# Spreading small transfers over six DMA engines and refilling the gaps around chunk six of a fused attention and spectral mixing kernel

## The chip, the cores and the metric

The program runs on one core of a Trainium2 chip. The metric is the device time of one execution in microseconds, as the median of several runs; every run computes the whole result.

## The reference

Eight sequences of 576 tokens pass through causal attention with eight heads of 64, and the result, seen as 512 channels, passes through a spectral layer. Cut to what matters:

```
cum    = cumsum(max(s, 0))                                   # per head, 576 values
scores = q k^T / 8 + min(cum_k - cum_q, 0), causal
x      = softmax(scores) v                                   # [8, 576, 512]
X      = rfft(x, over the tokens)[first 64 modes]
Y_m    = X_m (w_r[m] + i w_i[m])                             # one 512 x 512 complex product per mode
y      = irfft(Y)
u      = x + y
out    = u + max(u @ w_ch, 0)
```

The weights `w_r` and `w_i` are 64 matrices of 512 x 512 in fp32 each, 134 MB together. They are read once, and turned into bf16 by the transfer.

## The kernel before, in words

**The two stages.** The attention runs in 32 steps `n = (g, b)`: group `g` is one of four pairs of heads, that is 128 of the 512 channels, and `b` is the batch. Each step transposes q and k on TensorE (`transposes`), makes the scores and their exponentials (`scores`), multiplies with v (`av`), and takes the forward transform as a product with a table (`fft`). The running sums of `s` are needed as one more row of the transposed q: `cum_rows` (L336) brings two rows of 576 bf16 values from the DRAM tile `ncum_dram` into one partition of `qt`. SyncE issues these 30 small transfers.

**The weights.** A chunk `c` is eight modes. `modes(g, c)` (L470) multiplies the transformed x of group g with the chunk's weights: 16 products for `ri = 0` (`w_r`) and `ri = 1` (`w_i`), eight each. GpSimd issues all weight transfers in order (`load`, L243), usually 512 KB each and four for a chunk, into a ring of buffers. The products for groups 0 to 2 run between attention steps. Those of group 3, the last, run after attention, chunk by chunk, from 334 us on.

**What follows the last group.** For each chunk of group 3 the sum over groups is `y_sb` (VectorE, L502). `y_transposed` (L698) turns it on TensorE, `y_times_wch` (L706) multiplies with `w_ch` and gives `v_sb`. Both must get from "128 rows of (mode, batch)" into `yv`, with the mode on the partitions. For chunks 0 to 3 and part of 4 and 5 TensorE does it (`gather`); for `v_sb` of chunks 4 to 7 and `y_sb` of chunks 6 and 7 `spread` (L511) does it with a transfer from SyncE: 16 partitions of `yv`, eight pieces of 1 KB each.

**Work that doesn't need the weights.** The 18 output pairs (`pairs`, two tiles of 128 tokens each) need `x @ w_ch`. For 16 of them `keep` (L686) makes this product ahead of time and stores it with ScalarE (L539); six of these are made during attention, and the ten in `late` after it. `work` (L747) does one step of it: it transposes x for the next pair (`x_transposed`, L662: TensorE, then a VectorE copy per tile, through two PSUM buffers) and multiplies the pair before (`x_times_wch`, L677: eight products of 512 columns). The tuple `TAKE` says how many such steps follow each chunk, and `gather` of chunks 0 to 3 does two more. Pairs 0 and 1 stay in PSUM (`z_ps`, four banks, one for each parity and tile) and are finished first.

**The end.** The loop over chunks ends at L880; chunk 6 is L882 to L885. Chunk 7 is called with work between its four blocks of products:

```
yb = modes(NG - 1, NCK - 1, {2: lambda: (first_z(0), first_z(1)), 3: first_u})
```

The first two blocks need `w_r` of chunk 7, block three the first half and block four the second half of `w_i`. `first_z` (L893) adds the inverse transform of chunks 0 to 5 from `yv` and of chunk 6 from `v_sb` to pairs 0 and 1, and `first_u` (L888) does so for u of pair 0. After block four come `y_sb`, its transposition, `v_sb` of chunk 7, and then a written-out list of steps (L952 to L960) that finishes the 18 pairs and stores them. Instructions run on each engine in the order in which the program issues them; there is no scheduler.

Of the kernel before, what the change touches and what calls it, by code (L numbers as in the profile page):

```python
# [10 lines left out]
FP16 = mybir.dt.float16  # L11
BF16 = mybir.dt.bfloat16
# [6 lines left out]
def kernel(  # L19
# [11 lines left out]
    nc = tc.nc  # L31
    B, H, S, D = q.shape
    NM = moe_w_r.shape[0]
    DM = H * D
    P = 128
# [3 lines left out]
    NPAIR = B * H  # L39
    NG = DM // P  # L40
    DT = DM // P
# [4 lines left out]
    MC = 8  # L46
    NCK = NM // MC
# [12 lines left out]
    HP = P // 2  # L60
# [53 lines left out]
    auxpool = aux.enter_context(tc.tile_pool(name="aux_psum", bufs=2, space=PSUM, side="right"))  # L114

    dpool = ctx.enter_context(tc.tile_pool(name="dram", bufs=1, space=bass.MemoryType.DRAM))
    ncum_dram = dpool.tile([NPAIR, S + HP], BF16, name="ncum_dram")
    at = ExitStack()
    ap_ = at.enter_context(tc.tile_pool(name="attn", bufs=1))
    qkpool = at.enter_context(tc.tile_pool(name="qk_sb", bufs=2))  # L120
# [2 lines left out]
    ncum_sb = ap_.tile([NPAIR, S], BF16, name="ncum_sb")  # L123
    NQ = 2
# [211 lines left out]
    def cum_rows(n):  # L336
        if n >= N:
            return
        g, b = divmod(n, B)
        p0 = b * H + 2 * g  # L340
        if n >= 2:
            nc.sync.dma_start(out=qt[n % NQ][D : D + 1, :, :], in_=ncum_dram[p0 : p0 + 2, :S].unsqueeze(0))
            return
        for h in range(2):
            nc.sync.dma_start(out=qt[n % NQ][D : D + 1, h, :], in_=ncum_sb[p0 + h : p0 + h + 1, :])
# [124 lines left out]
    def modes(g, c, meanwhile=None):  # L470


        ps = auxpool.tile([P, DM], FP32, name="yp", tag="aux")
        cols = xs[g % 2].rearrange("p q k h r b m -> p q k (h r b) m")

        def product(ri, q_, cg):
            k0 = HP if ri == 1 and c == 0 and cg == 0 else 0
            nc.tensor.matmul(  # L478
                ps[32 * cg : 32 * cg + 32, :],
                cols[k0:, q_, 1 - ri, :, c * MC // 2 + cg],  # L480
                wt[(g, c, ri)][cg // 2][k0:, 2 * (cg % 2) + q_, :],
                start=(ri == 0 and q_ == 0), stop=(ri == 1 and q_ == 1),
                tile_position=(k0, 32 * cg), skip_group_check=True,
            )

        for x in range(4):
            ri, y = divmod(x, 2)
            if meanwhile and x in meanwhile:
                meanwhile[x]()
            for z in range(4):  # L490
                if meanwhile:
                    product(ri, z // 2, 2 * y + z % 2)
                else:
                    product(ri, y, z)
        if g == 0:
            nc.vector.tensor_copy(out=y_acc[:, c, :], in_=ps)
        elif g < NG - 1:
            nc.vector.tensor_tensor(out=y_acc[:, c, :], in0=ps, in1=y_acc[:, c, :], op=ALU.add)  # L498
        else:
            yb = spool.tile([P, DM], FP16, name="y_sb", tag="y")  # L500
            for cols in halves if c == NCK - 1 else [slice(0, DM)]:
                nc.vector.tensor_tensor(  # L502
                    out=yb[:, cols], in0=ps[:, cols], in1=y_acc[:, c, cols], op=ALU.add
                )
            if c >= NCK - 2:
                spread(c, 0, yb)
            return yb
# [2 lines left out]

    def spread(c, which, rows):  # L511

        nc.sync.dma_start(out=yv[16 * c : 16 * c + 16, :, which, :], in_=rows)

# [65 lines left out]
    with tc.tile_pool(name="sc_psum", bufs=2, space=PSUM) as scpool, \  # L582
            tc.tile_pool(name="tr_psum", bufs=1, space=PSUM) as trpool, \
            tc.tile_pool(name="av_psum", bufs=1, space=PSUM) as avpool:
        cum_rows(0)
        nc.sync.dma_start(out=ncum_dram[:, :S], in_=ncum_sb)
        transposes(0, 0)
        transposes(0, 1)
        load(loads_qk(2) + loads_v(2))
        pad_p()  # L590
        for n in range(N):
            if n in (0, 2):
                nc.vector.memset(xs_flat[n // 2].bitcast(FP32), 0.0)
            tails_due = loads_tails(n // B + 1)[n % B - 3 : n % B - 2] if 2 < n % B < 5 else []
            load((loads_qk(n + LA) if n % 2 else []) + loads_v(n + LA) + tails_due, loads_w(on_chip[n]))
            if n == N // 2 + 1:
                nc.gpsimd.dma_start(out=wch_sb, in_=moe_w_ch.rearrange("(dt p) e -> p dt e", p=P))
            cum_rows(n + 1)
            scores(n, 0)
            av(n - 1, 1)  # L600
            if n and n % B == 0:
                scores(n, 1)
                fft(n - 1)
                av(n, 0)
                mode_products(n, 0)
                transposes(n + 1, 0)
                mode_products(n, 1)
                transposes(n + 1, 1)
                continue
            mode_products(n)  # L610
            transposes(n + 1, 0)
            scores(n, 1)
            i = first_pairs[n - N + len(first_pairs)] if n >= N - len(first_pairs) else None
            if i is not None:
                first_transposed(i, 0)
            transposes(n + 1, 1)
            fft(n - 1)
            av(n, 0)
            if i is not None:
                first_product(i, 0)  # L620
                first_transposed(i, 1)
            if i is not None:
                first_product(i, 1)
        av(N - 1, 1)
        fft(N - 1)
# [11 lines left out]
    for b in range(4):  # L637
# [8 lines left out]
        old[:, i * 2 * DM : (i + 1) * 2 * DM].bitcast(FP16).rearrange("p (x t c) -> p x t c", x=2, c=P)  # L646
        for i in range(2)
    ]

    places = [finpool.tile([P, 4 * DM], BF16, name="r_sb", tag="r", bufs=3) for i in range(2)]  # L650
    places += [finpool.tile([P, 4 * DM], BF16, name=f"z1_{i}") for i in range(NLOC)]
# [8 lines left out]
        return [(slice(NL * i, NL * i + NL), b + i, ident16h[:NL, :NL]) for i in range(2)]  # L660

    def x_transposed(i):  # L662
        xts[i] = xt_sb[len(xts) % 2]
        for x, (b, T) in enumerate(pairs[i]):
            ps = upool.tile([P, DT, P], FP32, name="xt_ps", tag="u")
            for rows, bb, ident in parts(b, T):
                for dt in range(DT):
                    nc.tensor.matmul(
                        ps[:, dt, rows], x_all[: rows.stop - rows.start, dt, bb, T, :],
                        ident, start=True, stop=True, skip_group_check=True,  # L670
                    )
            nc.vector.tensor_copy(out=xts[i][:, x], in_=ps)
# [1 line left out]
    def start_z(i, x):  # L674
        zs[i, x] = zpool.tile([P, DM], FP32, name="z_ps", tag=f"z{i % 2}{x}")

    def x_times_wch(i, last):  # L677
        for x in range(2):
            start_z(i, x)
            for dt in range(DT):  # L680
                nc.tensor.matmul(  # L681
                    zs[i, x], xts[i][:, x, dt, :], wch_sb[:, dt, :],
                    start=(dt == 0), stop=(last and dt == DT - 1), skip_group_check=True,
                )

    def keep(i):  # L686
        x_times_wch(i, True)
        j = late.index(i)
        kept_place(i, places[j])
        for x in range(2):  # L690
            keep_product(i, x, zs.pop((i, x)))
# [6 lines left out]
    def y_transposed(yb, c=NCK):  # L698
        ps = auxpool.tile([P, DT, P], FP16, name="yt_ps", tag="aux")
        for dt in range(DT):  # L700
            nc.tensor.transpose(ps[:, dt, :], yb[:, bass.ts(dt, P)], ident16h)
        yt = yt_first[:, :, c % NY, :] if c < NCK - 2 else spool.tile([P, DT, P], FP16, name="yt_sb", tag="yt")
        nc.scalar.copy(out=yt, in_=ps)
        return yt

    def y_times_wch(c, yt):  # L706
        vp = auxpool.tile([P, DM], FP32, name="v_ps", tag="aux")
        for dt in range(DT):
            nc.tensor.matmul(
                vp, yt[:, dt, :], wch_sb[:, dt, :], start=(dt == 0), stop=(dt == DT - 1)  # L710
            )
        vb = spool.tile([P, DM], FP16, name="v_sb", tag="v")
        nc.vector.tensor_copy(out=vb, in_=vp)
        spread(c, 1, vb)
        return vb
# [41 lines left out]
            keep(i)  # L757

    late = [i for i in kept if i not in first_pairs]
    order_z = list(late)  # L760
    TAKE = (3, 2, 4, 0, 0, 0)
    us, rs = {}, {}
    last = len(pairs) - 1
    x_pool = ()
# [97 lines left out]
    for c in range(NCK - 2):  # L862
        yb = modes(NG - 1, c)
        for x in range(TAKE[c] - 1):
            work()
        if c == NCK - 3:
            x_transposed(0)
        yt = y_transposed(yb, c)
        if TAKE[c]:
            work()  # L870
        if c >= NY:
            if c == NCK - 3:
                x_times_wch(0, False)
                x_transposed(1)
            y_times_wch(c, yt)
            if c == NCK - 3:
                gather(NY, NCK - 2, (), (0,))
                x_times_wch(1, False)
        elif c == NY - 1:
            gather(0, NY, (1, 3), (1, 0))  # L880
    assert not order_z and not ahead
    c = NCK - 2  # L882
    yb6 = modes(NG - 1, c)
    yt = y_transposed(yb6)
    vb6 = y_times_wch(c, yt)  # L885


# [108 lines left out]
```

## Time and profile before

| what | value |
|---|---|
| median of 3 runs (range) | 441.62 us (440.95 to 442.1) |
| the profiled execution: time, span | 442.11 us, 440.3 us |
| mean granted TensorE clock | 0.925 |
| busy: TensorE, VectorE, ScalarE, GpSimd | 77%, 57%, 51%, 39% |
| HBM read, over the span | 163.58 MB, 393 GB/s with the writes |
| weight transfers of 512 KB, issue to landing | 13.6 us (`w_r`), 13.2 us (`w_i`) |
| chain that ended last: DMA, TensorE, VectorE | 53%, 25%, 15% |

The span runs from the first to the last instruction; the execution takes 1.8 us more than that. A DMA share of 1.1 in a window means that the 16 engines are busy throughout, since consecutive packets overlap a little. PEclk is the clock that TensorE was granted, 1.00 being full speed. The chain is followed back from the last instruction, so its shares say what ended the waits, not what an engine did in total.

### The profile page before, as it was taken

To read this page: it belongs to the slowest core of one execution; us is meant where nothing else is said; L and a number is where in the kernel's file an instruction comes from. 1 tells how busy PE (TensorE), PEld (TensorE's weight loads), DVE (VectorE), ACT (ScalarE), POOL (GpSimd) and SP (SyncE) were. 2 spreads that over 40 slices of the span, in tenths; PEclk is the share of its full clock that TensorE was granted. 3 is DMA by queue.
4 is the path that set the end of the run, shared out by engine and by line. 5 is a ranking of instruction groups with operands and counts; after the bars stand their busy time and mean duration, and the time that the engine had idled before them with its cause. 6 is when DMAs were issued, how large, how long until landed. Compare 5 with 4: busy or idle time off the path is not lost.

```text
span 440.3 us, 10592 instructions
## 1 busy us (share of the span) xinstructions
PE 340.8 (77%) x4409; PEld 203.7 (46%) x4409; DVE 252.5 (57%) x574; ACT 226.0 (51%) x421; POOL 171.7 (39%) x257
## 2 busy tenths in 40 slices
PE   1588999899695977973939458899987797778995
PEld 1365666465463644641616125556554345432341
DVE  7667776677573555752715315766655344450795
ACT  1387878267463634860727024766651334330794
POOL 6555454424353444323444343433322212310293
PEclk9999999999988888995968767999999989996999
DMA  9999999999999999999999999999999999996498
GB/s 179 207 206 206 204 206 208 207 209 207 207 205 207 210 207 210 207 209 208 205 209 208 209 208 209 207 210 206 210 211 212 212 211 211 203 218 121 155 381 347
DMA packets 69063, 93.30 MB, mean 212 GB/s; under 512 B 25932, under 2 KB 27592, under 8 KB 69016
## 3 DMA queue, kind: packets, MB, share of 16 engines
q0 software_dynamic: 61424, 81.28, 104.6%
q1 hardware_dynamic: 7592, 11.36, 7.2%
q8 instruction: 34, 0.56, 0.5%
q14 instruction: 13, 0.11, 0.1%
HBM read 163.58 MB, written 9.51 MB: 393 GB/s over the span
## 4 chain that ended last, share of the span: by engine, by line
DMA 53%; PE 25%; DVE 15%; issue 3%; POOL 2%; ACT 1%; DVEq 0%; POOLq 0%
DMA w_sb<-in_moe_w_i_dram 21%; DMA w_sb<-in_moe_w_r_dram 17%; DMA qk<-in_k_dram 8%; DMA qk<-in_q_dram 5%; PE sc_ps L397 3%; DVE xs L468 3%; DVE qt L359 3%; PE z_ps L681 3%; PE yp L478 3%; DVE x_all L443 2%; PE av_ps L433 2%; PE sc_ps L391 2%; PE tr_ps L355 2%; DVE xt L553 2%; PE z_ps L773 2%
## 5 line engine op out<-in xcount | busy, mean ns | idle before, releaser
L405 ACT ACTIVATE p_sb<-sc_ps,cumt_sb 128x576 f16<-128x576 f32 (+1 forms) x256 | 141.9, 636 | 21.8 <-PE sc_ps L397 21.4
L397 PE MATMUL sc_ps<-qt,kt 128*128 128x512 bf16 (+2 forms) x384 | 76.8, 312 | 6.9 <-ACT kt L359 6.1
L243 POOL DMA_DIRECT2D v<-in_v_dram x72 | 51.4, 714 | 60.6 <-DMA w_sb<-in_moe_w_i_dram 12.8
L243 POOL DMA_DIRECT2D w_sb<-in_moe_w_i_dram x62 | 38.5, 623 | 89.2 <-DMA w_sb<-in_moe_w_i_dram 28.3
L359 DVE COPY qt<-tr_ps 64x576 bf16<-64x576 bf16 x64 | 47.8, 747 | 41.5 <-PE tr_ps L355 41.5
L478 PE MATMUL yp<-w_sb,xs 128*32 128x512 bf16 (+1 forms) x480 | 42.2, 431 | 29.1 <-DMA w_sb<-in_moe_w_i_dram 25.4
L355 PE MATMUL tr_ps<-ident,qk 64*64 64x64 bf16 x1152 | 34.3, 205 | 33.8 <-DMA qk<-in_k_dram 16.0
L243 POOL DMA_DIRECT2D w_sb<-in_moe_w_r_dram x60 | 37.4, 624 | 53.0 <-DMA w_sb<-in_moe_w_r_dram 33.3
L397 PEld LDWEIGHTS <-kt 128*128 128x128 bf16 x384 | 38.3, 105 | 34.5 <-ACT kt L359 12.8
L391 PE MATMUL sc_ps<-negm,ident 128*128 128x256 bf16 x256 | 53.5, 293 | 0.1
L355 PEld LDWEIGHTS <-qk 64*64 64x64 bf16 x1152 | 26.4, 117 | 51.7 <-DVE kt L359 20.3
L376 ACT ACTIVATE p<-sc_ps,cumt 128x64 f16<-128x64 f32 x32 | 10.1, 314 | 73.8 <-PE sc_ps L372 73.6
L433 PE MATMUL av_ps<-v,p_sb 128*128 128x65 f16 x1024 | 44.2, 197 | 1.8 <-DVE x_all L443 0.6
L359 ACT COPY kt<-tr_ps 64x576 bf16<-64x576 bf16 x32 | 22.8, 714 | 40.8 <-DVE qt L359 40.1
L433 PEld LDWEIGHTS <-p_sb 128*128 128x128 f16 x1024 | 37.4, 100 | 9.6 <-DVE x_all L443 5.4
L468 DVE CAST xs<-ft_ps 64x128 bf16<-64x128 f32 x128 | 36.7, 287 | 7.3 <-PE ft_ps L458 5.7
L478 PEld LDWEIGHTS <-xs 128*32 128x32 bf16 (+1 forms) x512 | 17.8, 146 | 46.0 <-DMA w_sb<-in_moe_w_i_dram 24.6
L438 DVE TENSOR_REDUCE den<-av_ps 128x5 f32<-128x10 f32 x64 | 10.8, 169 | 48.3 <-PE av_ps L433 47.3
L443 DVE TENSOR_TENSOR x_all<-av_ps,rcp 128x320 f16<-128x320 f32 x64 | 31.5, 492 | 2.2
L498 DVE TENSOR_TENSOR y_acc<-yp,y_acc 128x512 f32<-128x512 f32 x16 | 11.1, 692 | 29.2 <-PE yp L478 28.5
L539 ACT COPY z<-z_ps 128x512 f32<-128x512 f32 x22 | 12.9, 586 | 26.9 <-PE z_ps L571 14.2
L458 PE MATMUL ft_ps<-Ff_sb,x_all 128*64 128x192 f16 (+1 forms) x320 | 24.4, 266 | 1.0 <-DVE x_all L443 1.0
(107 smaller groups left out, 439.4 us busy)
## 6 DMA issues: line engine op xcount, KB each, us to landing
w_sb<-in_moe_w_r_dram POOLq DMA_DIRECT2D x60, 512.0 KB, 13.6
w_sb<-in_moe_w_i_dram POOLq DMA_DIRECT2D x55, 512.0 KB, 13.2
out_dram<-r_w SPq DMA_DIRECT2D x16, 512.0 KB
v<-in_v_dram POOLq DMA_DIRECT2D x72, 64.0 KB, 11.1
qk<-in_q_dram POOLq DMA_DIRECT2D x15, 288.0 KB, 12.0
qk<-in_k_dram POOLq DMA_DIRECT2D x15, 288.0 KB, 13.2
x_all<-in_moe_w_r_dram POOLq DMA_DIRECT2D x4, 512.0 KB, 8.4
w_sb<-in_moe_w_i_dram POOLq DMA_DIRECT2D x3, 384.0 KB, 12.7
```

The source lines that it names most:

```text
L243: nc.gpsimd.dma_start(out=dst, in_=src)
L355: nc.tensor.transpose(ps[rows, r, :], src[rows, r, :], ident16[rows, rows])
L359: copy(out=to[:, :, :, half * RH : half * RH + RH], in_=ps[HP * i : HP * i + HP].rearrange("d r (h p) -> d h p r", h=2),)
L391: nc.tensor.matmul(ps[:, bass.ds(w * S, W)], ident16, negm[:, bass.ts(r, W)], start=True, stop=False, skip_group_check=True,)
L397: nc.tensor.matmul(ps[:, c0 : c0 + i1 - i0], keys[:, w, r, :], qh[:, i0:i1], start=False, stop=True, skip_group_check=True,)
L405: nc.scalar.activation(out=pt[:, poff[x] : poff[x] + S - w * W], in_=ps[:, w * S : (w + 1) * S - w * W], func=ACTF.Exp, bias=cumt_sb[:, x, ...
L433: nc.tensor.matmul(ps[:, I, r : r + NCH], lhsT, rhs, start=(i == 0), stop=(i == len(todo) - 1), skip_group_check=True,)
L443: nc.vector.tensor_tensor(out=x_all[:, g, b, :, D * h : D * h + D], in0=ps[:, :, 1 : NCH], in1=rcp.unsqueeze(2).to_broadcast([P, NT, D]), ...
L458: nc.tensor.matmul(ps[HP * q_ : HP * q_ + HP].rearrange("p h f -> p (h f)"), x_all[:nT, g, b, T, q_::2], Ff_sb[:nT, T, :], start=(T == 0), ...
L468: nc.vector.tensor_copy(out=xs[g % 2][HP * h : HP * h + HP, q_, :, h, :, b, :], in_=a)
L478: nc.tensor.matmul(ps[32 * cg : 32 * cg + 32, :], cols[k0:, q_, 1 - ri, :, c * MC // 2 + cg], wt[(g, c, ri)][cg // 2][k0:, 2 * (cg % 2) + ...
L681: nc.tensor.matmul(zs[i, x], xts[i][:, x, dt, :], wch_sb[:, dt, :], start=(dt == 0), stop=(last and dt == DT - 1), skip_group_check=True,)
```

## The change

It has two parts.

**Transfers.** `ncum_dram` is laid out as three pieces of 192 values per row, so that `cum_rows` moves six runs of 384 bytes instead of two of 1,152. `spread` cuts the 16 partitions of chunks 4 and 5 into three transfers of 6, 6 and 4 partitions; those of chunks 6 and 7 stay whole. By the change's own words these transfers then go over six DMA engines (pieces of 6 partitions or runs over six, the piece of 4 over four); two runs went over two, and 16 partitions over 16.

**Order.** One kept product, that of pair 17 (`late[-1]`), leaves the steps after chunk 2 (`TAKE[2]` goes from 4 to 3). Its transposition goes behind the products of chunk 5, ahead of that of pair 0, and its product with `w_ch` between the `w_r` blocks and the `w_i` blocks of chunk 6. The product of pair 1 moves from the end of chunk 5's part into chunk 6: one tile before the transposition of `y_sb`, one behind it. A third buffer, `xt_x`, holds transposed x. Giving `modes` a `meanwhile` also changes the order of chunk 6's products: two column groups at a time instead of four.

```diff
-    ncum_dram = dpool.tile([NPAIR, S + HP], BF16, name="ncum_dram")
+    NE6 = 6
+    CP = 2 * S // NE6
+    ncum_dram = dpool.tile([NPAIR, S // CP, CP + 32], BF16, name="ncum_dram")
...
-            nc.sync.dma_start(out=qt[n % NQ][D : D + 1, :, :], in_=ncum_dram[p0 : p0 + 2, :S].unsqueeze(0))
+            nc.sync.dma_start(
+                out=qt[n % NQ][D : D + 1, :, :],
+                in_=ncum_dram[p0 : p0 + 2, :, :CP].rearrange("h x t -> (h x) t"),
+            )
...
     def spread(c, which, rows):
-        nc.sync.dma_start(out=yv[16 * c : 16 * c + 16, :, which, :], in_=rows)
+        cuts = (0, 2 * MC) if c >= NCK - 2 else (0, NE6, 2 * NE6, 2 * MC)
+        for r0, r1 in zip(cuts, cuts[1:]):
+            nc.sync.dma_start(
+                out=yv[2 * MC * c + r0 : 2 * MC * c + r1, :, which, :], in_=rows[B * r0 : B * r1, :]
+            )
...
-        nc.sync.dma_start(out=ncum_dram[:, :S], in_=ncum_sb)
+        nc.sync.dma_start(
+            out=ncum_dram[:, :, :CP], in_=ncum_sb.rearrange("c (x t) -> c x t", t=CP)
+        )
...
+    xt_sb.append(finpool.tile([P, 2, DT, P], FP16, name="xt_x"))
...
-        xts[i] = xt_sb[len(xts) % 2]
+        xts[i] = xt_sb[len(xts) % 3]
...
-    def x_times_wch(i, last):
-        for x in range(2):
+    def x_times_wch(i, last, xx=(0, 1)):
+        for x in xx:
...
-    order_z = list(late)
-    TAKE = (3, 2, 4, 0, 0, 0)
+    order_z = late[:-1]
+    TAKE = (3, 2, 3, 0, 0, 0)
...
         if c == NCK - 3:
+            x_transposed(late[-1])
             x_transposed(0)
...
                 gather(NY, NCK - 2, (), (0,))
-                x_times_wch(1, False)
...
-    yb6 = modes(NG - 1, c)
+    yb6 = modes(NG - 1, c, {2: lambda: keep(late[-1])})
+    x_times_wch(1, False, (0,))
     yt = y_transposed(yb6)
+    x_times_wch(1, False, (1,))
     vb6 = y_times_wch(c, yt)
```

## The prediction

> **What bounds the kernel now.** I read the busy slices first. DMA is at 9 in every slice until 396 us, so the weights set the pace, and then there is a tail of 35 us. Second, the chain of waits around the hand-over, in order of time (start, length, what):
>
> ```profile
> 383.57 15.64 DMA w_sb<-in_moe_w_r_dram
> 399.21 0.14 issue
> 399.35 1.09 PE yp L478 x6
> 400.44 0.96 PE z_ps L773 x2
> 401.41 0.85 PE z_ps L784 x2
> 402.26 0.99 PE z_ps L773 x3
> 403.25 0.85 PE z_ps L784 x3
> 404.11 1.00 PE yp L478 x4
> 405.11 0.57 PE u_ps L803 x2
> 405.68 0.43 PE u_ps L773 x2
> 406.12 0.43 PE u_ps L784 x2
> 406.55 0.60 PE yp L478 x4
> 407.15 0.02 issue
> 407.17 0.44 DVE y_sb L502
> ```
>
> The `w_r` transfers of chunk 7 land at 399.21. From there TensorE, not DMA, holds the chain to the last products at 406.5. Two matmuls of 512 columns (L773) cost 0.96 at 400.44 and 0.43 at 405.68. Third, windows of 1 us and of one clock interval show why (PE, PEld, DVE, ACT, POOL busy; PEclk; DMA share; GB/s):
>
> ```profile
> 391.50:394.92 3.42, 2.22 (x21) 0.74 (x18) 2.38 (x4) 1.33 (x3) 0.00 (x0) 1.00 1.12 217
> 394.92:398.33 3.41, 1.43 (x8) 0.53 (x8) 1.08 (x2) 0.59 (x1) 0.00 (x0) 1.00 1.12 215
> 398.33:401.74 3.41, 2.39 (x12) 0.68 (x12) 0.00 (x0) 0.00 (x0) 0.00 (x0) 0.50 1.01 201
> 401.74:405.16 3.42, 3.42 (x15) 0.86 (x14) 0.00 (x0) 0.00 (x0) 0.00 (x0) 0.50 0.32 67
> ...
> 401.00:402.00 1.00, 1.00 (x3) 0.15 (x1) 0.00 (x0) 0.00 (x0) 0.00 (x0) 0.50 0.74 130
> 402.00:403.00 1.00, 1.00 (x5) 0.36 (x6) 0.00 (x0) 0.00 (x0) 0.00 (x0) 0.50 0.53 116
> 403.00:404.00 1.00, 1.00 (x6) 0.18 (x2) 0.00 (x0) 0.00 (x0) 0.00 (x0) 0.50 0.30 66
> 404.00:404.80 0.80, 0.80 (x6) 0.19 (x4) 0.00 (x0) 0.00 (x0) 0.00 (x0) 0.50 0.07 13
> ```
>
> TensorE was busy for 1.43 of 3.41 us ahead of 398.33, and then had half its clock until 405.16. And DMA does not stop at once: its share falls from 1.1 to 0.07, about one engine of 16, over 4 us. The engines reach the end of the same stream at different times; the last weights land at 404.80. Fourth, the queue table of the page names a load that isn't even:
>
> ```profile
> q8 instruction: 34, 0.56, 0.5%
> ```
>
> 34 packets take 0.5% of 16 x 440.3 us, 35 us, or 1.0 us each. 0.56 MB over TensorE's 8,818 instructions is 64 bytes each, so I take them for fetches of its code. Their lengths in the trace's DMA records repeat with a period of eight (974, 961, 893, 892, 948, 945, 935, 974 ns), so I read eight engines in turn, each made late by some 4 us. Between 354 and 384 us the completions of 512 KB transfers form 16 series with a step of 2.486 us each, which is an engine at its own limit, not a shared one. At 325 to 330 us these series stand in two groups: eight within 2.3 us of the earliest, eight 2.8 to 4.6 us behind it.
>
> **Part 1, the transfers.** A spread costs each of 16 engines eight packets of 1 KB. These took 59 ns in the records, less 19 ns by which consecutive packets overlap: 8 x 0.040 and a completion, 0.35 us. By the queue row of SyncE (7,592 packets, 7.2%, 67 ns each) it would be 0.53. Two spreads leave the late engines, if these are not among the six: the end of the weights moves from 404.8 to 404.1, and `w_r` of chunk 7 from 399.2 to 398.5. Bounds: if the late engines are among the six, they get 16 packets more per spread, 2 x 16 x 0.040 = 1.3 us later; at best 2 x 0.53 = 1.1 us earlier. I take 0.7 earlier: around the last running sum, at 310.0, which goes over the two engines of the old layout, two series that stretch by 61 ns belong to the early group. This places two of the six; the other four I assume.
> The running sums: 30 x 2 packets of 1,152 bytes, 61 ns each by those series, become 30 x 6 of 384 bytes, 22 ns (the records of the 384-byte pieces of the table loaded at the start) to 44 with a completion. Two engines save 30 x 17 to 39 ns, 0.5 to 1.2 us, four others gain 0.7 to 1.3; these are ahead of the late ones by more than that. Nobody waits for these rows (the list of who held up TensorE names transposes and ScalarE, no transfer of `qt`), so this costs nothing unless they come a whole step, 6.6 us, later. The store into `ncum_dram` has 12 packets per engine x 22 ns instead of 4 x 64: equal. SyncE issues four more transfers at 0.55 us each; queued behind them are the next spreads, whose data comes 4 us later, and the stores: nothing. `v_sb` of chunk 7 reuses chunk 5's buffer and so waits for three pieces (399.2 below, written at 406): nothing.
> A row weighed against a rule: the DMA share above falls over 4 us, so dealing evenly over 16 would keep the late ones late. The Trainium skill (DMA: Bandwidth & Descriptors, Rules for kernel authors) speaks against the change: it asks for an outermost dimension that is a multiple of 16, since a smaller one confines a transfer to as many engines. By the rule alone the 0.7 would be 0, and the sum 1.6.
>
> **Part 2, the order.** The kept product leaves the stretch after chunk 2: 0.45 (xt_ps) and 1.73 (z_ps) on the chain, 2.2 us. Chunk 5 started at 383.38 without a wait for data. Its weights: chunk 6's last wait ended at 393.91; four transfers of 2.486 are 9.94, a fetch 1.0 and a spread 0.35 lie between: 382.6. So of the 2.2 only 0.8 is gained there; the rest turns into waiting for weights.
> Chunk 5 then gets two more transposes. TensorE's part is 0.6, but four tiles pass two buffers, each freed by a VectorE copy of 0.65 behind `y_sb` (0.69): `x_times_wch(0)`, queued behind the waiting transposes with `y_sb`'s own, starts 2.85 us after the products, not 1.4. The gather ends at 390.5 - 0.8 + 1.4 = 391.1, and the 1.9 of pair 1 is gone from there. Chunk 6: `w_r` products, two groups at a time, 0.9, to 392.0; the kept product 1.73, to 393.7, over the time in which TensorE waited 0.79 for `w_i`; `w_i` products to 394.6; pair 1's first tile 0.86 under `y_sb` (0.80 waited before); the second under ScalarE's copy (0.68 waited before); `v_ps` 1.04, to about 397.8. `v_sb` follows at 398.5; `first_z` needs it only at 400.
> So the interval ahead of the hand-over holds nearly 3 us of work instead of 1.43, and the idle stretch before chunk 7 is 0.7 instead of 1.87. With the clock kept: `w_r` 398.5 + 0.14; 0.9 of products; `first_z` at half its 3.65, 1.85; block three 0.5; `first_u` 1.3: 403.2. Block three finds its half of `w_i` (two transfers of 1.25 before the last: 401.6) just there. Block four then waits for the weights at 404.1 + 0.1 = 404.2, against 406.48: **2.3 us**. That is the next late thing: without part 1's 0.7 it is 404.9, 1.6 us. With half the clock it is 398.5 + 7.13 (406.48 - 399.35) = 405.6, 0.9 us.
> Does the clock stay? Row: 1.43 busy of 3.41 halved it; 391.50 to 394.92 had 2.22 busy and did not. Between these I take the nearer, 2.22, for an interval with 2.2 or more in any phase. The intervals run on their own grid, so a run may fall otherwise.
> The Trainium skill (TensorE: Matmul & The Clock Gate, Part 1) has the gate throttle after an idle window of 3.4 us; here the window wasn't idle, so the row goes further than the rule. By the rule there would have been no loss to win back, and the sum would be part 1 alone.
> From block four on the tail is the same instructions, TensorE bound with its clock up in both, so the gain passes 1:1. ScalarE's two more copies (0.59 each) in chunk 6 lie in its idle time (it waited 3.4 and 2.1 us there); they free the banks of pair 1 at 393.5 and 394.3, ahead of 394.6. Without that cover pair 1 would come up to 0.6 later, within the 1.0.
>
> **Sum.** The profiled execution took 442.11 (440.3 and 1.8 around it), 0.5 above the median. 442.11 - 2.3 = 439.8; from the median it is 439.3. Some of the runs before may have kept their clock, which would explain their 1.15 us of spread, so I stay near the first: **439.7**.
>
> **Rivals.** A measurement tells 0.3%, 1.3 us, from no change.
> (a) The six engines are no help or only the clock is won: 1.6 us, 440.0 to 440.5. For it: no row gives the engine of a packet.
> (b) The clock halves anyway: 0.9 us, 440.8 to 441.2. For it: 2.39 busy of 3.41 did not bring it back at 401.74.
> (c) The six engines include late ones: weights end at 404.8 + 1.3 = 406.1, block four 0.3 earlier than before: 441.3 to 441.8.
> (d) Slower: the spread of chunk 5 becomes the late one. Its three pieces put 24 packets on four engines, each between two weight packets of 0.154: 24 x 0.19 = 4.6 us from 394.6 (issue 390.7, and 3.9 us from issue to packets, as the spreads at 384.2 and 395.3 show): 399.2, when `first_z` wants it at 399.6. It decides from 400.6 on (the 1.0 by which block four waits anyway). With one packet per two of the weights it is 24 x 0.35 = 8.3, 402.9; TensorE stands still for over 3 us, the clock halves, and `first_z` 3.65, block three 1.07 and `first_u` 1.45 end at 409.1: +2.6, 444.2 from the median. Against it: packets alternate one for one in the records at 400.
>
> **How the numbers follow.** The forecast gets 0.48, (a) 0.18, (b) 0.12, (c) 0.08, (d) 0.14. Faster by over 0.3% (under 440.3): the forecast and half of (a), 0.57. Within: half of (a), (b), (c), 0.29. Slower: 0.14. The range goes from 438.8 (part 1 at 1.1, from the median: 441.62 - 2.7) to 441.9, past (c); (d) is outside. The forecast's own range is 438.8 to 440.3.
>
> **What would show it.** Right: PEclk 1.00 from 395 to 405; L773 at 0.43 per two; a wait of block four for `w_i` of about 1 us; the last weights at 404.1, with the DMA share steeper; a small wait ahead of chunk 5. Wrong: a wait of L773 for `yv` (d); 0.50 in PEclk (b); weights that end at 404.8 or later (a, c); new waits for `qt` in the attention steps.

## The result, and the profile after

The change makes the kernel slower: 443.16 us (median of 22 runs, 441.38 to 445.27) against 441.74 us (22 runs of the kernel before beside it). The ratio is 1.003, with a 95% interval of 1.0019 to 1.0041: 0.8 to 1.8 us. The forecast of 439.7 and its range up to 441.9 both miss it. The profiled execution took 443.24 us, with a span of 441.5 and a mean clock of 0.913, close to the median.

The chain of waits of the kernel after, at the places shown of before (start, length, what):

```profile
347.29 15.89 DMA w_sb<-in_moe_w_i_dram
...
363.22 0.69 PE yp L483 x8
...
392.33 0.42 PE g_ps L740 x16
...
402.88 0.60 PE yp L483 x8
403.48 0.54 PE z_ps L785 x2
404.02 0.43 PE z_ps L796 x2
404.45 0.55 PE z_ps L785 x4
405.01 0.43 PE z_ps L796 x4
405.44 0.58 PE yp L483 x4
406.02 0.54 PE u_ps L815 x2
...
407.43 0.60 PE yp L483 x4
408.05 0.44 DVE y_sb L507
```

From 363.22 on no piece of this chain is a weight transfer. Block four, which began at 406.55 before, begins at 407.43, and it waits for TensorE: the last weights landed at 404.5 by the trace's DMA records (404.8 before). The two products of L773, now L785, cost 0.54 instead of 0.96, so the clock is up at the end, as forecast, and yet the end is 0.9 us later. The windows show what came ahead of that (PE, PEld, DVE, ACT, POOL busy; PEclk; DMA share; GB/s):

```profile
361.00:364.34 3.34, 1.27 (x17) 0.36 (x16) 0.41 (x1) 0.59 (x1) 1.22 (x2) 1.00 1.14 213
364.34:374.58 10.24, 8.26 (x49) 5.35 (x50) 4.16 (x7) 2.81 (x6) 1.22 (x2) 0.50 1.12 211
374.58:395.06 20.48, 15.06 (x164) 8.77 (x162) 10.00 (x17) 7.04 (x13) 4.83 (x8) 1.00 1.08 203
395.06:398.47 3.41, 3.00 (x13) 0.95 (x14) 1.73 (x3) 0.85 (x3) 0.00 (x0) 0.50 1.13 216
398.47:408.00 9.53, 9.53 (x62) 3.38 (x60) 1.38 (x2) 1.70 (x3) 0.00 (x0) 1.00 0.56 118
```

In this execution the clock halves at two other places, from 364 to 375 and from 395 to 398, and each time TensorE holds the chain. Which intervals fall so differs between executions; that alone is no cause. What the change does to the time had to come from runs with its parts taken singly.

### The profile page after: what moved, and what is told of

It reads as the page before. It is cut to its first block, busy times and chain, and to the rows that moved or that the text cites. A ratio compares the mean times of both kernels' runs of the same rounds, so it can differ in the third digit from the quotient of the medians.

```text
span 441.5 us, 10548 instructions
## 1 busy us (share of the span) xinstructions
PE 340.1 (77%) x4362; PEld 205.1 (46%) x4409; DVE 252.6 (57%) x574; ACT 226.1 (51%) x421; POOL 171.3 (39%) x257
## 4 chain that ended last, share of the span: by engine, by line
DMA 44%; PE 30%; DVE 17%; issue 3%; ACT 3%; POOL 2%; DVEq 0%; POOLq 0%; ACTq 0%
DMA w_sb<-in_moe_w_i_dram 18%; DMA w_sb<-in_moe_w_r_dram 16%; DMA qk<-in_k_dram 5%; PE yp L483 5%; DVE qt L364 4%; PE z_ps L693 4%; DVE xs L473 3%; PE sc_ps L402 3%; DMA qk<-in_q_dram 3%; PE tr_ps L360 2%; DVE x_all L448 2%; PE av_ps L438 2%; PE sc_ps L396 2%; DVE kt L364 2%; PE g_ps L740 2%
## 5 line engine op out<-in xcount | busy, mean ns | idle before, releaser
L402 PE MATMUL sc_ps<-qt,kt 128*128 128x320 bf16 (+2 forms) x337 | 65.2, 297 | 10.7 <-ACT kt L364 5.8
L364 DVE COPY kt<-tr_ps 64x576 bf16<-64x576 bf16 x32 | 24.4, 762 | 0.4
```

What stands on the lines that cost most here:

```text
L364: copy(out=to[:, :, :, half * RH : half * RH + RH], in_=ps[HP * i : HP * i + HP].rearrange("d r (h p) -> d h p r", h=2),)
L402: nc.tensor.matmul(ps[:, c0 : c0 + i1 - i0], keys[:, w, r, :], qh[:, i0:i1], start=False, stop=True, skip_group_check=True,)
```

## The experiments

All were timed in five rounds beside the kernel before. Differences in us are the ratio less one, times the median of before in the same rounds; in brackets the 95% interval. The ratio takes in every execution, so it need not follow the medians where single executions are long (`order_spreads` below). Each profile is of one execution.

**Each part alone.** `order_only` has the second part (order) and the transfers of before; `transfers_only` the running sums and both spreads, with the order of before.

```diff
# transfers_only, beside the new layout of ncum_dram
-        nc.sync.dma_start(out=yv[16 * c : 16 * c + 16, :, which, :], in_=rows)
+        cuts = (0, 2 * MC) if c >= NCK - 2 else (0, 6, 12, 2 * MC)
+        for r0, r1 in zip(cuts, cuts[1:]):
+            nc.sync.dma_start(out=yv[2 * MC * c + r0 : 2 * MC * c + r1, :, which, :], in_=rows[B * r0 : B * r1, :])
# order_only
-    order_z = list(late)
-    TAKE = (3, 2, 4, 0, 0, 0)
+    order_z = late[:-1]
+    TAKE = (3, 2, 3, 0, 0, 0)
...
-    yb6 = modes(NG - 1, c)
+    yb6 = modes(NG - 1, c, {2: lambda: keep(late[-1])})
+    x_times_wch(1, False, (0,))
     yt = y_transposed(yb6)
+    x_times_wch(1, False, (1,))
```

> Only the running sums and the spreads of chunks 4 and 5 go over six engines; the order of the work is that of before. Theory O (the order costs the time: with the kept product gone from the stretch after chunk 2 TensorE waits for the weights of chunk 3, its clock halves during the gather, and it never again gets ahead of the weights): 0 to 0.5 us faster than before, since the last weights land a little earlier (404.4 against 404.8 in the two profiles). Theory T (the transfers cost it: the attention ended 0.46 us later in the changed kernel, first products of the last group at 334.63 instead of 334.17): 1.0 to 1.5 us slower.

> Only the order is changed: the kept product of pair 17 from chunk 2 to chunk 6, and pair 1 into chunk 6; the transfers are those of before. Theory O: 1.2 to 2.0 us slower than before, with a half clock from about 364 us on and no wait of TensorE for weights after chunk 3. Theory T: 0.5 us faster to no change, and chunk 7 waits for its weights.

Measured: `transfers_only` 444.17 us, +2.6 (+1.6 to +3.5); `order_only` 440.82, -0.9 (-1.8 to -0.1). The order helps, and the transfers cost more than it brings, and more than theory T expected. In `order_only` the clock stayed up over the hand-over, and the chain ends on the weights, as the forecast had it for part 2 alone:

```profile
394.92:398.33 3.41, 3.41 (x25) 1.36 (x23) 1.39 (x2) 1.52 (x3) 0.00 (x0) 1.00 1.15 221
398.33:401.74 3.41, 2.93 (x19) 1.08 (x18) 0.69 (x1) 0.59 (x1) 0.00 (x0) 1.00 0.99 191
```

```profile
388.20 17.48 DMA w_sb<-in_moe_w_i_dram
405.68 0.04 issue
405.72 0.67 PE yp L478 x4
```

In `transfers_only` TensorE starts on the `w_r` of chunk 7 at 400.53 instead of 399.35, and behind their products there is a gap that the profile puts down to nothing:

```profile
383.89 16.51 DMA w_sb<-in_moe_w_r_dram
400.40 0.14 issue
400.53 1.09 PE yp L480 x6
401.62 0.57 issue
402.20 1.01 PE z_ps L779 x2
```

L779 is the inverse transform in `first_z`, which reads `yv`. The trace's semaphore events, by which each DMA engine reports that its share of a transfer has landed (sixteen for a whole spread, six for a piece of six partitions), explain the gap: the last piece of chunk 5's spread is complete at 402.00. This is the first sign of rival (d).

**The smallest piece of the order.** `pair1_moved` only moves the product of pair 1 into chunk 6 and leaves the kept product where it was.

```diff
-                x_times_wch(1, False)
...
+    x_times_wch(1, False, (0,))
     yt = y_transposed(yb6)
+    x_times_wch(1, False, (1,))
```

> Only the product of pair 1 moves into chunk 6, on both sides of the transposition of y_sb; the kept product stays behind chunk 2, the transfers are those of before. Theory O: chunk 3 is as before, TensorE waits some 2.5 us for the weights of chunk 6 instead of 0.8 and the product fills the 0.7 behind it; 0.5 us faster to 0.5 us slower, depending on whether the clock stays up through that wait. Theory T: the same. The third reading: 1 to 1.5 us slower.

Measured: 440.68 us, -0.8 (-1.5 to -0.2), no worse than the whole order. Its profiled execution had half the clock from 392.4 to 399.2 and still began block four at 405.08. The other half, the kept product moved without pair 1 (`keep_moved`), has no time: pair 17 needs the two banks of `z_ps` that pair 1 then still holds, and the engines wait for each other for ever.

**Which of the transfers.** `sums_only` has the running sums over six engines, `spreads_only` the two spreads in pieces of 6, 6 and 4, `spreads_eight` the two in two pieces of 8 (`cuts = (0, 8, 2 * MC)`).

> The two spreads in three pieces (6, 6 and 4 partitions), running sums and order as before. So far: both transfer edits together cost 2.4 us (441.8 to 444.17), with the last w_r of chunk 7 at 400.53 instead of 399.21 and the last weights at 405.46 instead of 404.80. Theory S (the six engines include the late ones: 16 packets of 1 KB more per spread on these at 0.04 us, 2 x 16 x 0.04 = 1.3 us, and the pieces of chunk 5 come late for first_z): slower by 1.5 to 2.4 us, w_r of chunk 7 at 400.2 or later. Theory R (the running sums in six packets of 384 bytes cost it): within 0.5 us of before, w_r of chunk 7 at 399.2 to 399.6.

> The running sums and their store in runs of 384 bytes over six engines, spreads and order as before. Theory S: within 0.5 us of before (four engines gain 30 x 22 to 44 ns = 0.7 to 1.3 us, two lose 0.5 to 1.2), w_r of chunk 7 at 399.0 to 399.6. Theory R: slower by 1.5 to 2.4 us, and w_r of chunk 7 at 400.2 or later.

> A dose between: the two spreads in two pieces of 8 partitions, which puts 16 packets on each of eight engines instead of 24 on four and 16 on two (before: 8 on each of sixteen). Theory S: an engine that is late gets 8 packets more per spread instead of 16, so about half of the loss of the three pieces, slower by 0.6 to 1.2 us, w_r of chunk 7 about 0.6 later than before. Theory R: within 0.5 us of before.

Measured: `sums_only` 441.66, +0.3 (-0.2 to +0.8); `spreads_only` 442.81, +1.5 (+0.8 to +2.1); `spreads_eight` 442.55, +1.4 (+0.7 to +2.1). The spreads cost it. Two pieces cost about as much as three, which the dose of theory S did not foresee. The landing of `w_r` of chunk 7, on which theories S and R are also set, tells nothing: in the profiles of all runs it is at 398.79 to 400.40 with split spreads and at 398.69 to 400.37 without.

**Which spread.** `split_four` cuts only chunk 4's spread (`c != NCK - 4` keeps the others whole), `split_five` only chunk 5's (`c != NCK - 3`).

> Only the spread of chunk 4 in three pieces (6, 6, 4); it is through by 392, and first_z reads it at 400, so it cannot be late for a reader. Theory W: half of the loss of both spreads, +0.4 to +0.9 us. Theory L (chunk 5's spread, late for first_z, costs it): within 0.3 us of before.

> Only the spread of chunk 5 in three pieces. With chunk 4's at 0.0 and both at +1.3, chunk 5's alone should cost +0.9 to +1.5 under theories W and L alike; a smaller cost (under 0.5) would say that the two spreads only cost together, by what they add up to on the same six engines.

Measured: `split_four` 441.46, 0.0 (-0.5 to +0.5); `split_five` 443.72, +1.9 (+1.0 to +2.9). Chunk 5's carries it all, and by its middle more than was expected. Its chain, and one row of the list of who held up TensorE, name the wait:

```profile
390.71 0.77 SPq L515
391.48 0.05 issue
391.52 9.58 DMA yv<-v_sb
401.10 0.05 issue
401.15 1.04 PE z_ps L777 x2
```

```profile
PE z_ps L777 <- DMA yv<-v_sb: 0.6, 1, 0.6
```

The last piece is issued at 391.5 and `first_z` gets it at 401.1. The DMA records show how: the sixteen engines of before finished this spread together, at 395.5 to 396.2. Here six finish the first piece at 395.4 to 396.2, six the second at 397.5 to 398.3, four the third at about 399.2 to 399.9 (the records don't name the engine, so single packets can belong to the next spread). That is one packet of 1 KB in 0.21 to 0.25 us, which fits a turn with about one weight packet. Another 1.2 us pass until the last of the four engines reports the landing, at 401.10; the whole spread of before had landed at 396.42, 0.3 behind its last packet. The wait of 0.6 that the trace shows is a part of the 1.9: this execution, at 442.91, is 0.8 under its run's median.

**Is it the six engines' load?** `load_six` keeps the spreads whole and lets two more transfers follow each, 6 x 8 packets of 1 KB into spare DRAM; `load_sixteen` the same 96 KB over all sixteen; `load_five` has those of `load_six` behind chunk 5 only; `tiny_five` two transfers of 16 x 64 bytes behind chunk 5.

```diff
         nc.sync.dma_start(out=yv[16 * c : 16 * c + 16, :, which, :], in_=rows)
+        if c < NCK - 2:                                   # load_five: c == NCK - 3
+            for r0 in (0, 6):
+                nc.sync.dma_start(out=spare[c % 2, r0 : r0 + 6, :B, :DM], in_=rows[B * r0 : B * (r0 + 6), :])
```

> The two spreads stay whole over sixteen engines; two more transfers of 6 x 8 packets of 1 KB follow each of them, into spare DRAM that nobody reads: 16 packets more on each of six engines, twice. Theory W (the six engines include those that set the landing of the weights; 2 x 16 x 0.04 = 1.3 us): slower by 0.8 to 1.6 us, as the spreads in pieces were (+1.25). Theory L (the pieces are only late for first_z, or hold up the spreads behind them, and the weights do not mind): the copies also stand ahead of the later spreads in SyncE's queue, so within 0.6 us of before, and the last weights within 0.3 of 404.8.

> The same two extra transfers per spread and the same 96 KB as load_six, into spare DRAM, but each over all sixteen engines (6 packets more on each instead of 16 on six). Theory W (the load of the six engines costs it): the latest engine gets 2 x 6 x 0.04 = 0.5 us, so +0.2 to +0.6, less than half of load_six (+1.0). Rival (the number of transfers or their bytes cost it, whatever the engine): +0.8 to +1.2, as load_six.

> The two extra transfers on six engines follow chunk 5's spread alone; all spreads stay whole, so no reader gets its rows late. Theory W, with the place that split_four points to (only what comes late in the stream counts): +0.7 to +1.2, as load_six. Theory L (lateness of chunk 5's own pieces): 0 to +0.3.

> The kernel before with two more transfers behind chunk 5's spread, of 16 packets of 64 bytes each, into spare DRAM that nobody reads: transfers without bytes. If the number of transfers costs it (SyncE's queue, its rings): +0.7 to +1.2 us as with load_five. If it is the bytes: 0.0 within 0.4.

Measured: `load_six` 442.55, +1.3 (+0.7 to +1.9); `load_sixteen` 443.0, +1.3 (+0.7 to +2.0); `load_five` 442.28, +0.9 (+0.2 to +1.7); `tiny_five` 442.44, +0.6 (0.0 to +1.1). The same bytes cost the same on six engines and on sixteen, so theory W, that the choice of engines delays the weights, falls; it fell with `split_four` already. But theory L did not foresee a cost of the copies either, since nobody waits for them. An estimate by bytes fits the intervals of the three copies: 96 KB at the 216 GB/s of the windows is 0.45 us for each spread. That a transfer without bytes costs nothing isn't settled by `tiny_five`. The change adds no bytes to the spreads, but like `tiny_five` it puts two more transfers behind chunk 5's first, so part of what its split costs may be due to their number, a rival that stays open (`split_four` adds two as well, behind chunk 4's, and cost nothing).

**Inside the change.** `order_sums_six` is the change without the split spreads, `order_spreads` without the new running sums, `after_whole_five` without chunk 5's split alone:

```diff
-        cuts = (0, 2 * MC) if c >= NCK - 2 else (0, NE6, 2 * NE6, 2 * MC)
+        cuts = (0, 2 * MC) if c >= NCK - 3 else (0, NE6, 2 * NE6, 2 * MC)
```

> The change without its spreads: the new order and the running sums over six engines. Theory S (the spreads alone cost): as the order alone, 440.8, which is 0.5 to 1.2 us faster than before. Rival (running sums and order together cost, as running sums and spreads together seemed to cost 0.9 more than the sum of the two alone): 441.5 or above.

> The change without its running sums: the new order and the spreads in pieces. Theory S: nearly the whole loss against the order alone, 442.1 to 443.2, slower than before by 0.5 to 1.5 us. Rival (the running sums carry most of it inside the change): 441.0 to 441.6, faster than before or the same.

> The whole change except that chunk 5's spread stays one transfer over sixteen engines. Theory L (the last piece of chunk 5's spread reaches first_z at about 401 instead of 397): the loss goes, to what the order with the running sums had, 440.7 to 441.6, at or below before. Rival (the loss comes from all parts together): 442.3 or above, at most a third of the 1.5 us gone.

Measured: `order_sums_six` 441.01, -0.2 (-0.8 to +0.3); `order_spreads` 441.20, +0.4 (-0.4 to +1.1); `after_whole_five` 441.51, 0.0 (-0.5 to +0.6), inside what theory L expected. Leaving chunk 5's spread whole takes the change from +1.3 to nothing. `order_spreads` missed what theory S expected of it: its median lies in the rival's range, under the 441.55 of before beside it, and its ratio is above one through single executions of up to 444.30. Its profile, of its fastest execution, shows the late piece again, with TensorE early and its clock up:

```profile
399.15 0.67 PE yp L478 x8
399.82 1.00 issue
400.82 0.59 PE z_ps L778 x2
```

The third piece's packets end at about 399.6 there, and it has landed at 400.62 by the semaphore events, 0.2 before 400.82. `after_whole_five` has no such gap, and its chain ends on the weights, as in `order_only`:

```profile
388.49 17.09 DMA w_sb<-in_moe_w_i_dram
405.57 0.04 issue
405.62 0.67 PE yp L483 x4
```

**The parts added up.** The runs hold every combination of the three parts. In the four pairs that differ by one part alone, the split spreads add 1.5, 2.3, 1.3 and 1.5 us, the running sums 0.3, 1.1, 0.7 and 0.9, and the order -0.9, -0.5, -1.1 and -1.3. The means, 1.65, 0.75 and -0.95, add up to the change's +1.3 within 0.2, so the parts seem to act each by itself. If the intervals are independent, each mean is good to about 0.5 (an estimate from the intervals above).

**What the clock is worth.** `before_fill7` and `before_fill4` add eight and four matmuls of 512 columns behind `v_ps` of chunk 6 to the kernel before; nobody reads them.

```diff
     vb6 = y_times_wch(c, yt)
+    filler(1, 8)          # before_fill4: 4
```

> The kernel before with eight more matmuls of 512 columns, whose result nobody reads, after v_ps of chunk 6, in the time in which TensorE waits for w_r of chunk 7: 1.7 us at full clock. It tells what the clock alone is worth at the end. Theory C (the interval with 1.43 us busy of 3.41 halves the clock, which then costs the chain): PEclk 1.00 from 398 to 405, block four waits for its weights at about 404.9 instead of starting at 406.55, faster by 1.0 to 1.6 us. Rival (the end is set by the transfers, whose last lands at 404.80, and the clock hides behind them; or the added products push w_r's own): within 0.5 us of before or slower.

> The kernel before with four more matmuls of 512 columns (0.9 us at full clock) after v_ps of chunk 6, result unread. Theory C (the halved clock ahead of chunk 7 costs the chain): 34 code fetches as before, PEclk 1.00 from 398 to 405 in most runs, faster by 0.6 to 1.5 us. Rival (clock hidden behind the transfers): within 0.4 us of before.

Measured: 442.38, +1.2 (+0.6 to +1.8), and 441.96, +0.8 (-0.1 to +1.6). The expectation failed in the time, but not at its place. In the profile of `before_fill7`, its fastest execution, the clock was up from 399.5 on:

```profile
400.37 0.60 PE yp L478 x8
400.97 0.54 PE z_ps L781 x2
...
404.91 0.60 PE yp L478 x4
...
434.00 0.60 DVEq L1000
```

Block four begins at the forecast 404.9, and the last piece of the chain, on VectorE's queue, starts at 434.00 instead of 435.65. But the queue table counts one more fetch:

```profile
q8 instruction: 35, 0.57, 0.5%
```

By the records it runs for 1.43 us at 430.8, amid the last stores. In the last microsecond of these 13 packets follow one another, as on one engine, where in before 139 end, and the stores end at 439.0 (439.1 before). So the 1.6 us that the clock brought went to an engine that was late with the end. That the fetch made it late is argued, since the records don't name the engine. `before_fill4` has 34 fetches within its span, but its profiled execution, at 445.68 us, is the slowest of its twelve and says nothing of the usual one. In it the four matmuls did not keep the clock, which was halved from 396.5 to 403.4.

## Why the prediction was wrong

**Part 1, the transfers: the step that failed.** It gave the two spreads a gain of 0.7 us, with bounds of -1.1 to +1.3, because packets leave the late engines. Measured alone they cost 1.5 us, past the upper bound by its middle (the interval, 0.8 to 2.1, takes it in), and chunk 5's alone 1.9. No gain in the weights appeared: their last landing lies between 403.6 and 405.5 in the runs with split spreads, at 404.8 in before. The assumption that the six engines are not the late ones found no support either: where chunk 4's pieces pass in `transfers_only`, the two latest of the series of completions stretch and nine others keep their step of 2.486 us. But by `split_four` even that costs nothing that could be measured.

**Rival (d) named the place and got 0.14.** Its price for one packet in turn was 24 x 0.19 = 4.6 us from 394.6, so 399.2, and it decides only from 400.6 on; so I took the rows of the spread to come in time. Two terms were too small. Packets took 0.21 to 0.25 us each (394.6 to 399.6 in `order_spreads`, 393.9 to 399.9 in `split_five`). And the end of the packets was taken for the arrival, with 1.0 to 1.2 us missing in these two runs. With both, 24 x 0.23 + 1.2 = 6.7 from 394.6 gives 401.3, beyond that point. The price of 2.6 us lies inside the interval of `split_five` by luck: it took the piece to come at 402.9 and TensorE to stand still for over 3 us, and measured were 401.1 and 0.6.

The Trainium skill (DMA: Bandwidth & Descriptors, Anatomy of one DMA) puts a fixed cost of some 2.0 us on a transfer issued by GpSimd, most of it the wait for the write's receipt behind the last byte. The 0.3 to 1.2 us between last packet and landing here, on transfers of SyncE, agree in kind and are smaller. The rule cited against the change (same page, Rules for kernel authors) was the better guide: each piece of six partitions shows landings from just six engines.

**The running sums** were priced at nothing: +0.3 alone, not told from zero. Yet in all four pairs that differ by them alone the run that has them is slower, by 0.75 on the mean, so nothing was probably too low. Where this arises no run shows.

**Part 2, the order,** was right in kind. Forecast without part 1: 1.6 us, block four waiting for weights at 404.9. Measured: 0.9 (0.1 to 1.8), waiting for weights at 405.7, as the last of them came 0.6 later in that execution. So the end of the weights is one mis-sized term. A step ahead of it was wrong: the 1.9 us of pair 1 is not "gone from there". In before, its product (390.50 to 392.40) ran while VectorE copied the gathered rows out of PSUM, and the products of chunk 6 need these buffers. Without it TensorE waits just as long, and the `w_r` products of chunk 6 begin at 393.99 in `order_only` (forecast 391.1) and at 395.47 in the change. The rows of `order_only` and of the change:

```profile
PE yp L478 <- DVE yv L739: 1.9, 1, 1.9
PE yp L483 <- DVE yv L750: 1.9, 1, 1.9
```

`order_only` had room for this, since block four waited for weights anyway; the change had not. One sum is off by a little too: 441.62 - 2.7 is 438.9, not 438.8.

**The clock** was expected to stay up where the interval ahead of the hand-over is filled. It did in the profiled executions of `order_only`, `order_spreads` and `after_whole_five`. It did not in that of the change (395.06 to 398.47) and, with 0.56 and 0.58 from 394 to 398, in that of `order_sums_six`, where the intervals fell otherwise. So rival (b)'s mechanism is there in some executions. Nor is 2.2 us of work in an interval enough in any phase: in the change's execution 2.45 us from 333.60 to 337.03 were followed by half the clock.

**In the changed kernel itself** the late piece hides behind a late TensorE. Chunk 5's `v_sb` is written 3.0 us later than before (392.38 against 389.35), after the half clock of 364 to 375 and the added transposes; the packets of its spread run from 397.2 to 402.3, and its last piece has landed at 403.07 by the semaphore events. `first_z` begins at 403.42, without a wait for it. So with the spread issued when it was, a TensorE that was in time could have begun at most 0.4 us earlier. That is worked out, not shown by a run.

**What stays open.** Why two pieces of eight partitions cost 1.4 us: in the one profile, the fastest of its twelve runs, they are not late for a reader (landed at 397.83, read at 399.68). In the profile of `spreads_only` too the last piece lands at 400.51, ahead of `first_z` at 401.17. So the wait is shown in three profiles (`transfers_only`, `split_five`, `order_spreads`, 0.6 to 1.0 us each), and what the split costs beyond it, the number of transfers perhaps, is not. And how much of the change's loss is the late piece, how much the two clock stretches: `after_whole_five` gives back 1.3 us, and `order_only` stands 0.9 further down, with intervals that touch.

**The version that beats both** is the order alone (440.82) or only pair 1 moved (440.68), with the spreads left over sixteen engines.

## What to carry to other kernels

Price a small transfer by the arrival of its last packet at its reader, not by the bytes that it takes from others: packets on its fullest engine, times the turn that each takes beside the bulk stream, and the time until its landing is reported (0.3 to 1.2 us here). Cutting a transfer that someone waits for into pieces for fewer engines lengthens just that. And when a gain at a place vanishes at the end, look for the new last thing on the chain, be it one engine of sixteen.

## What the runs showed of the hardware

- From the last packet of a spread to the landing that its reader waits for: 0.3 us for chunk 5's in before (396.15 to 396.42), 1.2 in `split_five`. In `before_fill4` one engine's packets of chunk 7's `y_sb` end at 412.16 (the others' at 410.4 to 410.7), and TensorE goes on at 413.35:

```profile
408.74 4.61 DMA yv<-y_sb
413.35 0.04 issue
```

  The records show a fetch of 1.63 us at 409.7 ahead of it, and that engine's eight packets start at 411.30, when the fetch ends (411.31): a fetch of TensorE's code can sit before a packet that TensorE itself waits for.
- The 10.24 us at half clock in the change's execution are three intervals of 3.41, with 2.39, 2.46 and 3.41 us busy, and the clock came back behind the third. The Trainium skill (TensorE: Matmul & The Clock Gate, Part 1) speaks of some 3.4 us of sustained work for that, which agrees here. It isn't always enough: in `split_four` the interval from 334.39 was busy throughout, and the next was still at half. The 1.34 busy of 3.41 us before 364.34 did not keep the clock.
- In the profile of `before_fill7`, with sixteen more instructions on TensorE (eight matmuls and their weight loads), there is a 35th code fetch, in the last 10 us.
